# First weights' parts made earlier, matrix parts loaded over 15 steps, and three more places for second weights, in a two-layer spectral and MLP kernel

## The chip, the cores and the metric

The kernel runs on one core of one Trainium2 chip. The metric is the device time of one execution in microseconds; before the change it is 2771.64 us, the median of three runs (2771.27 to 2773.43). The engines are TensorE (PE, with its weight loads as PEld), VectorE (DVE), ScalarE (ACT), GpSimd (POOL) and the queue from which all DMAs are issued (SP). Each engine works through its own instructions in program order. An instruction that needs another engine's result, or a place that another still reads, waits on a semaphore, and everything behind it on that engine waits too.

## The reference

The input x has 2048 tokens (S) of 576 features (D). Two layers follow each other, with the same weights in both:

```python
x = x + _A_ref(_layernorm(x), ...)     # y = Cr @ (z @ Dr.T) - Ci @ (z @ Di.T), with z the normalized x
x = x + _B_ref(_layernorm(x), ...)     # y = gelu(layernorm(z) @ w1 + b1) @ w2 + b2
x = x + _A_ref(_layernorm(x), ...)
x = x + _B_ref(_layernorm(x), ...)
```

Cr and Ci are 2048 x 2048 (the sequence matrices), Dr and Di 576 x 576 (the hidden matrices), w1 is 576 x 4608, w2 is 4608 x 576; all of it is float32.

## The kernel before

**Arithmetic.** Every operand of a matmul is cut into a high and a low part (`split`, or an ACT copy followed by a DVE subtraction), and a product is three matmuls: high by high, high by low, low by high (`PASSES`). The large products use a Strassen-like scheme with seven block products in place of eight (`ORDER`, `OUTER`), so sums and differences of blocks have to be made as well.

**Stages.** For each layer:

- *Sequence products* (`Sequence`). `fill` normalizes x and makes the right sides. `run` then goes through 14 token tiles t of 128 rows (the first two are done in `first_mms`), each with seven products i of 24 matmuls of 288 columns, 98 in all. In each of the 98 steps DVE and ACT also prepare the cell (high and low part of a block of Cr and Ci) that is used some steps later: `high` (line 554), `low`, and the block sums `sums`. `post` moves results on and stores a token tile's product UV to DRAM.
- *Token-tile stage* (`hidden`, from line 777), for half 0 and half 1 of the tokens, eight tiles each. For each tile UV is transposed on PE (`turn`, line 764), multiplied with the nine 128-row parts of the hidden matrices (`dd`), added to x, normalized (`norms`) and transposed again (`turn_y`, line 834). The matrix parts are made in layer 0, half 0, and stored (`keep_d`); the three later times they are loaded, 576 KB for each of the nine.
- *MLP of that half* (`mlp`). 18 feature tiles q, worked in nine pairs g. `inner(q)` is a tile's first product: seven block products (the orders of `ORDER`) of seven matmuls, 512 columns wide, 49 matmuls, then gelu. `outer(g, i, side)` is one second product: two halves jj of 12 matmuls of 288 columns, 24 in all. In a pair's turn stand inner(2g), then outer(g-1) for i = 1, 6, 5, 3 (96 matmuls), inner(2g+1), then outer(g-1) for i = 7, 4, 2 (72). The last pair has outer only (g = NG).

**Weights' parts.** The seven block combinations of w1, each in high and low part, are made once, by the generator `weights()` (lines 247 to 294), in the background. A *step of the maker* is one resumption: low part of one combination (DVE subtraction of 384 columns, its store to `w1s`, for four of seven combinations a POOL sum or difference of 384 columns, and at times a load of raw w1) and high part of the next (two ACT copies). It takes 129 resumptions to its end. `pump()` is one resumption; `tick(share)` resumes in `share` of four calls. Before, `Sequence.run` calls tick(3) after each of the 98 products, and `inner` calls tick(2) after each of the seven orders. All of this falls into layer 0, half 0; afterwards the background is empty and both calls do nothing. When the maker ends, it frees its staging place, columns 0 to 1920 of the memory R.

The seven combinations of w2 are made in the MLP of layer 0, half 0, for pair g during turn g+1 (`make`, `due`, `advance`; hi is ACT, line 957, lo is DVE with a store to `w2s`). They go straight into the places that outer reads (`c2`). All later MLPs load them from `w2s`, 576 KB each, whenever a place is idle (`load_w`).

**Places.** In half 0, `c2` has two places, and a third (`give1`) when two of the seven places of first weights (`c1`) are given up. In half 1 it has three from the start. Taking and giving is first in, first out, in program order.

**Loads for half 1.** `Hidden.steps` (from line 685) is a generator that `outer` resumes in the last pair (g = NG-1), once for each jj, 14 times. It places the UV tiles and the matrix parts into the memory of Y, which is free when the last `inner` is done.

The program on SP is the order in which these calls are made; nothing reorders it.

Of the kernel before, what the change touches and what calls it, by code (L numbers as in the profile page):

```python
# [16 lines left out]
NT = S // P  # L17
# [136 lines left out]
def spectral_mixer(ctx: ExitStack, tc: tile.TileContext, x, dh, c0, cs, w1, b1, w2, b2, out):  # L154
# [149 lines left out]
    def tick(share):  # L304

        ticks[0] += 1
        if ticks[0] * share % 4 < share:
            pump()
# [6 lines left out]
    class Sequence:  # L315
# [286 lines left out]
        def run(self, hidden):  # L602
            for p in range(NP):
                while self.ready <= p:
                    next(self.pieces)
                self.first_mms(p)

            for _ in self.pieces:
                pass
            hidden.reserve()  # L610
            if not self.early:

                for k in range(KH):
                    dma(dhd[k], dh[k])
            steps = self.steps
            self.low(*steps[1])
            self.high(*steps[2])
            for t in range(PLAIN):
                self.first_post(t)
            for n, (t, i) in enumerate(steps):  # L620
                self.load_c()
                if n + 2 < len(steps):
                    self.low(*steps[n + 2])
                if i == 2 and t + 1 < NT:
                    self.sums(t + 1)
                self.load_c()
                if n + 3 < len(steps):
                    self.high(*steps[n + 3])
                self.mms(t, i)
                self.post(t, i)  # L630
                if t == NT - 1:
                    hidden.begin(self, ORDER.index(i))
                tick(3)
            for k in range(2):
                self.L[k].free()
            self.own.close()
            for z in self.Z:
                z.free()
            hidden.take()


    class Hidden:
# [41 lines left out]

        def steps(self):
            self.uvs = Slots(R, 2, 2 * D, Y_AT[0])
            self.X = A.place(X_AT[1], NT * DH)
            self.places = [R.place(Y_AT[0] + 4 * D + k * 2 * D, 2 * D) for k in range(KH)]

            def load_d(k):  # L690
                b = self.places[k].at
                self.load_d(k, Block(R, b, D), Block(R, b + D, D))

            self.load(0)
            load_d(0)
            yield
            self.load(1)
            load_d(1)
            for k in range(KH):
                yield  # L700
                if k + 2 < KH:
                    load_d(k + 2)
                self.high_d(k)
                if k:
                    self.low_d(k - 1)
            yield
            self.low_d(KH - 1)
            drain(self.turn(0, R.place(UT_AT[1][0], 2 * KH * P)))
            self.load_uv(2)
            yield  # L710
# [66 lines left out]
    def hidden(h, mlp):  # L777
# [74 lines left out]
        for n in range(NP):  # L852
            h.load(n + 2)
            for k in (n,) if n < NP - 1 else (n, n + 1):
                h.keep_d(k)
            if n:
                drain(turn(n + 1), *ln)
            if n == NP - 3:
                next(mlp)
            o = space()  # L860
            if n == NP - 1:

                h.uvs.close()
                next(mlp)
                o, ring = pp[0], [2, 3] * 3
            u = h.ut.pop(n)
            for k in range(KH):
                if n == 0 and k == KH // 2:
                    drain(turn(1))
                for m, (a, b) in enumerate(PASSES):  # L870
                    for e in range(2):
                        mm(o[:, e, :DH], u(2, KH, P)[:, a, k], h.dd[k][b](2, DH)[:, e],
                           k == 0 and m == 0, k == KH - 1 and m == 2)
            u.free()
            clock[0] += 1
            tile_x = xv[:, :, order[n]]
            add(nc.vector, tile_x, o[:, :, :DH], tile_x)
            if n >= 3 and n % 2:
                rests((n - 3) // 2)
            g = norms(n)  # L880
            next(g)
            ln = [g]
            if n >= 3 and n % 2:
                y_steps = turn_y((n - 3) // 2)
                if n < NP - 1:
                    drain(y_steps)


        for _ in range(3):
# [21 lines left out]
    def mlp(hid, store, first, after):  # L911
# [186 lines left out]
        def outer(g, i, side):  # L1098
            for jj in range(2):
# [14 lines left out]
                work(slot[0] % 3 < 2 or g >= last - 1)  # L1114
                slot[0] += 1
                advance()
                if g == last:
                    next(after, None)
                to = goal[i][:, 2 * jj:2 * jj + 2]
                if i == 6 and g == 0:  # L1120
# [24 lines left out]
        for g in range(NG + 1):  # L1145
# [2 lines left out]
                due.extend(make(g - 1))  # L1148
            if g == NG:
                work(99)  # L1150
                c1.close()
                hs.close()
                Y.free()
            for f in range(2):
                if g < NG:
                    for _ in inner(2 * g + f, None if g or f else 1):
                        pass
                if g:
                    advance(6 + 15 * f)
                    at[0] = 7 + 15 * f  # L1160
                    slot[0] = 0
                    for i in OUTER[f]:
                        outer(g - 1, i, 1 - f)
# [81 lines left out]
```

## Time and profile before

| what | value |
|---|---|
| runs (median, lowest, highest) | 2771.64, 2771.27, 2773.43 us |
| profiled execution: its own time | 2771.1 us |
| its span, first to last instruction | 2769.3 us |
| mean granted TensorE clock | 0.995 |
| DMA | 543.74 MB, mean 196 GB/s |

A line of the profile gives the kernel line, the engine, the operation, out<-in by the program's names, sizes (partitions x elements), a count and busy time. L194 and L191 are the helpers `sub` and `add`, L201 the helper `mm`, L188 the helper `dma`, so that all subtractions have one line, and the sizes tell them apart. R and A are the two large memories, bank is the accumulators, w_parts stands for both `w1s` and `w2s`. In a row of stretches stand, after the stretch and its length, the busy time of PE, PEld, DVE, ACT and POOL, each with its count of instructions, the granted share of the TensorE clock, the share of DMA engines busy and GB/s. Square brackets at the end of a row of the timeline hold the wait ahead of the instruction and what ended it. Neighbouring instructions of a stretch's edge are counted with it, so that the 49 matmuls of a first product are shown as 50 to 52.

The stages begin at these times of the span: sequence products of layer 0 at 67.7 us, token tiles of half 0 at 376.6, MLP at 464.2, token tiles of half 1 at 908.0, MLP at 996.2; sequence products of layer 1 at 1469.1, token tiles of half 0 at 1777.0, MLP at 1864.2, token tiles of half 1 at 2271.2, MLP at 2359.5.

### The profile page before, as it was taken

The numbers are of one execution on the slowest core, as the hardware profiler recorded it, in microseconds if no ns is written. First come the engines' busy times: TensorE is split into PE (matmuls) and PEld (weight loads), VectorE is DVE, ScalarE is ACT, GpSimd is POOL, SyncE is SP. The second block draws the span as 40 slices with busy tenths as digits, with TensorE's granted clock in tenths as the row PEclk, the third lists the DMA queues.
The fourth block names the chain that finished last, engine by engine and source line by source line (L and its number), as shares of the span: only waits on it lengthen the run. The fifth ranks groups of instructions, "written<-read, shape, count | busy, mean of one in ns | idle before, by whom it ended". The sixth has DMA issues, their size and how long they took to land.

```text
span 2769.3 us, 45580 instructions
## 1 busy us (share of the span) xinstructions
PE 2684.4 (97%) x17596; PEld 2513.2 (91%) x17596; DVE 1756.6 (63%) x2566; ACT 1087.4 (39%) x1850; POOL 791.9 (29%) x762
## 2 busy tenths in 40 slices
PE   7999999999999999999989999999999999999999
PEld 7999998788888988989889999998999989998988
DVE  8788866777776465555577666555555544655555
ACT  6555544544443243333254333334333313433331
POOL 5222223544534332222251000042222224221222
PEclk9999999999999999999999999999999999999999
DMA  5666675777776546666553333526666663566664
GB/s 198 240 222 223 231 257 172 268 263 271 263 262 216 216 152 195 192 196 192 168 206 119 124 126 125 187 98 208 194 195 192 189 247 132 185 194 195 191 197 152
DMA packets 208712, 543.74 MB, mean 196 GB/s; under 512 B 21985, under 2 KB 56801, under 8 KB 208353
## 3 DMA queue, kind: packets, MB, share of 16 engines
q1 hardware_dynamic: 208496, 540.84, 58.7%
q8 instruction: 139, 2.28, 0.3%
q14 instruction: 77, 0.62, 0.1%
HBM read 428.69 MB, written 114.72 MB: 196 GB/s over the span
## 4 chain that ended last, share of the span: by engine, by line
PE 69%; DVE 5%; issue 3%; DMA 3%; POOL 2%; ACT 1%; SPq 0%; POOLq 0%; DVEq 0%; ACTq 0%
PE bank L201 68%; DVE R L194 2%; DMA R<-w_parts 1%; DVE A L191 1%; POOL A L194 1%; DMA A<-x_mid 1%; PE bank L764 1%; POOL R L194 1%; DMA w_parts<-R 0%; DVE bank L191 0%; DVE A L194 0%; DVE moments L216 0%; DVE moments L231 0%; ACT R L957 0%; ACT R L1073 0%
## 5 line engine op out<-in xcount | busy, mean ns | idle before, releaser
L201 PE MATMUL bank<-R 128*128 128x288 f32 (+2 forms) x16972 | 2624.9, 316 | 72.3 <-DVE A L191 23.3
L201 PEld LDWEIGHTS bank<-R 128*128 128x128 f32 x16972 | 2447.5, 189 | 240.9 <-DVE A L191 30.3
L191 DVE TENSOR_TENSOR A<-bank,A 128x576 f32<-128x576 f32 (+3 forms) x808 | 567.4, 710 | 613.5 <-PE bank L201 533.6
L194 POOL TENSOR_TENSOR R<-A,R 128x512 fp32r<-128x512 f32 x288 | 374.3, 1310 | 981.5 <-ACT R L1073 948.6
L194 DVE TENSOR_TENSOR R<-A,R 128x1024 fp32r<-128x1024 f32 (+4 forms) x449 | 447.3, 1024 | 44.7 <-ACT R L554 25.4
L191 POOL TENSOR_TENSOR A<-A 128x576 f32<-128x576 f32 (+2 forms) x102 | 131.1, 1287 | 639.0 <-ACT A L592 349.6
L1013 ACT ACTIVATE bank<-bank,b1t 128x512 f32<-128x512 f32 (+1 forms) x224 | 144.8, 646 | 373.8 <-DVE bank L191 253.6
L194 DVE TENSOR_TENSOR R<-bank,R 128x512 fp32r<-128x512 f32 (+4 forms) x408 | 251.6, 636 | 59.7 <-ACT R L197 50.2
L1073 ACT ACTIVATE R<-A 128x512 fp32r<-128x512 f32 x288 | 176.2, 628 | 276.4 <-DVE A L194 117.3
L554 ACT ACTIVATE R<-A 128x1024 fp32r<-128x1024 f32 x196 | 204.0, 1054 | 135.4 <-DVE A L194 105.5
L191 DVE TENSOR_TENSOR bank<-bank,A 128x512 f32<-128x512 f32 (+1 forms) x228 | 152.2, 670 | 152.1 <-PE bank L201 151.7
L194 POOL TENSOR_TENSOR A<-A 128x288 f32<-128x288 f32 (+2 forms) x170 | 200.6, 1193 | 154.9 <-DVE R L194 83.9
L197 ACT ACTIVATE R<-bank 128x512 fp32r<-128x512 f32 (+2 forms) x160 | 74.1, 514 | 185.6 <-PE bank L764 129.3
L1073 ACT ACTIVATE R<-bank 128x512 fp32r<-128x512 f32 x216 | 120.7, 595 | 32.0 <-PE bank L201 32.0
L194 DVE TENSOR_TENSOR A<-A 128x1024 f32<-128x1024 f32 (+2 forms) x116 | 127.7, 1106 | 4.3 <-ACT A L241 1.2
L1040 ACT ACTIVATE A<-bank 128x512 f32<-128x512 f32 (+1 forms) x76 | 43.7, 575 | 211.6 <-PE bank L201 208.9
L241 ACT ACTIVATE A<-A,moments 128x576 f32<-128x576 f32 x64 | 54.0, 868 | 113.0 <-POOL moments L224 80.7
L194 DVE TENSOR_TENSOR A<-bank,A 128x512 f32<-128x512 f32 x144 | 98.2, 682 | 0.0
L594 DVE SCALAR_TENSOR_TENSOR A<-A 128x288 f32<-128x288 f32 x28 | 18.4, 657 | 88.4 <-POOL A L191 88.4
L1013 ACT ACTIVATE A<-bank,b1t 128x512 f32<-128x512 f32 (+1 forms) x76 | 50.4, 663 | 54.8 <-DVE bank L191 54.8
L268 ACT ACTIVATE R<-A,power,middle 128x128 fp32r<-128x128 f32 x126 | 60.8, 483 | 0.0
L222 POOL TENSOR_TENSOR moments<-moments,power 128x1 f32<-128x1 f32 x32 | 17.6, 551 | 148.3 <-DVE moments L219 148.3
(50 smaller groups left out, 632.4 us busy)
## 6 DMA issues: line engine op xcount, KB each, us to landing
R<-w_parts SPq DMA_DIRECT2D x504, 320.0 KB, 3.3
R<-w_parts SPq DMA_DIRECT2D x189, 576.0 KB, 3.7
A<-in_cs SPq DMA_DIRECT2D x112, 512.0 KB, 4.3
w_parts<-R SPq DMA_DIRECT2D x126, 320.0 KB, 3.7
w_parts<-R SPq DMA_DIRECT2D x63, 576.0 KB, 4.0
uv_mid<-A SPq DMA_DIRECT2D x32, 576.0 KB, 2.8
A<-in_w SPq DMA_DIRECT2D x72, 192.0 KB, 3.8
R<-dh_parts SPq DMA_DIRECT2D x23, 576.0 KB, 10.5
```

The costliest lines, as they stand in the source:

```text
L191: engine.tensor_tensor(dst, a, b, op=op)
L194: engine.tensor_tensor(dst, a, b, op=OP.subtract)
L197: nc.scalar.activation(hi, src, AF.Copy)
L201: nc.tensor.matmul(o, a, b, start=start, stop=stop, skip_group_check=True)
L241: nc.scalar.activation(dst, src, AF.Identity, bias=mv[:, 4:5], scale=mv[:, 3:4])
L268: nc.scalar.activation(t[:, 2], src[:, 1], AF.Identity, bias=power[:, 2:3], scale=middle)
L554: nc.scalar.activation(self.cells[t, i](2, NP, P)[:, 0], self.source(t, i), AF.Copy)
L594: nc.vector.scalar_tensor_tensor(uv[:, 1, 0], p7, -1.0, u, op0=OP.mult, op1=OP.subtract)
L764: nc.tensor.transpose(at, v[:, k], ident)
L1013: nc.scalar.activation(dst, src, AF.Gelu_apprx_tanh, bias=bias(f))
L1040: nc.scalar.activation(up, o, AF.Copy)
L1073: nc.scalar.activation(H[q, k](2, TC)[:, 0], src, AF.Copy)
```

## The change

There are three parts.

1. The maker's steps. `Sequence.run` resumes the maker after every one of the 98 products (before after three in four), and `hidden` resumes it twice at the end of each token tile. In the MLP `inner` still resumes it after every second order, for as long as it lasts.
2. Loads for half 1. `Hidden.steps` is resumed six times in the second group of the second-to-last pair's turn (outer(NG-2), i = 7, 4, 2) and then 14 times as before. First come the first UV tile and the nine matrix parts, one for each resumption, with the second UV tile after the third; then the two x tiles; the transposition of UV tile 0 stands in the 17th resumption, one order's half earlier than before. `high_d` and `low_d`, which did nothing when the parts are only loaded, are no longer called. To have room, the memory of Y and the places of first weights are given up right after the last `inner`, and no longer at the start of the last turn.
3. Places for second weights in half 0. A fourth one is taken at columns 0 to 1152 of R as soon as these are free (in layer 0 when the maker has ended, in layer 1 from the first turn), and two more in the memory of the first weights when those are given up.

```diff
@@ Sequence.run
-                tick(3)
+                pump()
@@ Hidden.steps
             self.uvs = Slots(R, 2, 2 * D, Y_AT[0])
-            self.X = A.place(X_AT[1], NT * DH)
             self.places = [R.place(Y_AT[0] + 4 * D + k * 2 * D, 2 * D) for k in range(KH)]
-
-            def load_d(k):
+            self.load_uv(0)
+            for k in range(KH):
                 b = self.places[k].at
                 self.load_d(k, Block(R, b, D), Block(R, b + D, D))
-
+                yield
+                if k == 2:
+                    self.load_uv(1)
+            self.X = A.place(X_AT[1], NT * DH)
             self.load(0)
-            load_d(0)
             yield
             self.load(1)
-            load_d(1)
-            for k in range(KH):
+            for _ in range(6):
                 yield
-                if k + 2 < KH:
-                    load_d(k + 2)
-                self.high_d(k)
-                if k:
-                    self.low_d(k - 1)
-            yield
-            self.low_d(KH - 1)
             drain(self.turn(0, R.place(UT_AT[1][0], 2 * KH * P)))
@@ hidden, end of each token tile
+            pump()
+            pump()
@@ mlp, outer
-                if g == last:
+                if g == last or half == 0 and g == last - 1 and side == 0:
                     next(after, None)
@@ mlp, turns
             if g == NG:
                 work(99)
-                c1.close()
                 hs.close()
-                Y.free()
+            if half == 0 and len(c2.idle) < 4:
+                more = R.place(0, 4 * DH)
+                if more:
+                    c2.idle.append(more)
             for f in range(2):
                 if g < NG:
                     for _ in inner(2 * g + f, None if g or f else 1):
                         pass
+                if g == last and f:
+                    c1.close()
+                    Y.free()
+                    if half == 0:
+                        c2.idle += [R.place(C1_AT[0] + k * 4 * DH, 4 * DH) for k in range(2)]
```

## The prediction

> **What bounds the kernel now.** The first page gives the balance of the engines, and the stretches of the span, cut at the first matmul of each stage, give the place of every loss.
>
> ```profile
> span 2769.3 us, 45580 instructions
> PE 2684.4 (97%) x17596; PEld 2513.2 (91%) x17596; DVE 1756.6 (63%) x2566; ACT 1087.4 (39%) x1850; POOL 791.9 (29%) x762
> ```
>
> TensorE (PE) is the bound, so a change can win only where PE waits or runs slowly. The same work stands in the span twice, once for each layer, which gives a yardstick: layer 0 makes weights' parts beside it, layer 1 doesn't. The view of busy time by stretch, columns PE, PEld, DVE, ACT, POOL, granted clock, DMA share and GB/s:
>
> ```profile
> 67.71:376.59 308.88, 308.58 (x2329) 308.11 (x2330) 252.72 (x275) 168.80 (x304) 74.44 (x54) 1.00 0.68 230
> 1469.09:1777.01 307.92, 307.92 (x2329) 307.92 (x2329) 196.78 (x204) 119.34 (x158) 11.69 (x14) 1.00 0.38 136
> 376.59:464.20 87.61, 84.34 (x656) 82.79 (x655) 48.72 (x105) 32.88 (x67) 33.95 (x58) 1.00 0.53 184
> 908.87:996.16 87.29, 83.74 (x648) 81.96 (x647) 44.37 (x96) 27.57 (x58) 33.39 (x57) 1.00 0.43 149
> 464.20:907.97 443.77, 412.79 (x2381) 364.36 (x2378) 319.17 (x462) 204.75 (x390) 195.10 (x143) 0.99 0.74 262
> 1864.19:2271.21 407.02, 401.53 (x2380) 363.60 (x2378) 228.12 (x344) 130.52 (x219) 98.49 (x77) 1.00 0.64 202
> ```
>
> Rows 1 and 2 are the sequence products of layers 0 and 1: the maker's steps beside layer 0 cost PE 1 us. Rows 3 and 4 are the token-tile stage without and with nothing of the maker either. Rows 5 and 6 are the MLP of half 0: 443.77 against 407.02 us, a loss of 36.8 us in layer 0. Cut finer, in three parts and by single products:
>
> ```profile
> 464.20:515.11 50.91, 44.12 (x254) 37.67 (x251) 36.73 (x61) 29.17 (x61) 24.52 (x20) 1.00 0.82 282
> 1864.19:1906.32 42.13, 42.13 (x253) 38.02 (x251) 27.37 (x46) 20.22 (x37) 11.70 (x10) 1.00 0.68 205
> 634.41:646.89 12.48, 11.63 (x51) 9.23 (x50) 8.88 (x11) 7.38 (x15) 7.40 (x6) 1.00 0.63 218
> 828.40:839.98 11.58, 11.58 (x52) 9.30 (x51) 6.48 (x9) 5.59 (x9) 5.88 (x4) 1.00 0.57 192
> 854.51:866.06 11.55, 11.51 (x52) 9.15 (x50) 5.53 (x8) 4.35 (x7) 0.00 (x0) 1.00 0.54 186
> 1972.42:1983.80 11.38, 11.38 (x52) 9.32 (x51) 4.14 (x6) 3.64 (x6) 2.54 (x2) 1.00 0.70 204
> 866.06:907.97 41.91, 33.56 (x218) 32.12 (x216) 24.29 (x32) 9.36 (x15) 17.88 (x13) 0.88 0.69 260
> 2235.05:2271.21 36.16, 30.87 (x217) 30.20 (x216) 17.39 (x25) 4.79 (x9) 11.40 (x9) 0.95 0.81 309
> ```
>
> The start (tiles 0 to 2) loses 50.91 - 42.13 = 8.8 us; the end loses 41.91 - 36.16 = 5.8 us; what lies between, 515.11 to 866.06 against 1906.32 to 2235.05, loses 350.95 - 328.73 = 22.2 us. Rows 3 to 6 are single first products (the 49 matmuls of one feature tile). With the maker's steps one takes 12.48 us, and PE is busy for 11.63 of them; tiles 16 and 17, after the maker has ended, take 11.58 and 11.55 although the second weights are still made beside them; in layer 1 it is 11.38. So 0.91 us of a product is the maker, 0.2 the second weights.
>
> **The change, part by part.**
>
> *Maker's steps.* It needs 129 resumptions. Before, three in four sequence products give 73, and every second of 7 orders in a tile gives 3.5 per tile, so tiles 0 to 15 carry the other 56. After, 98 sequence products give 98, eight token tiles 16, and 15 are left for tiles 0 to 4. Twelve first products (4 to 15) lose their steps, the last few of them not wholly burdened: 12 x 0.91 = 10.9, of which I take **-10**, since the lighter of them (tile 15, half empty) lost less. The 96 matmuls between them barely change (I take -1). Start: tiles 0 to 3 keep their steps, **0** (bounds -4 and +4, half of the 8.8 either way, because the steps fall on other orders).
>
> Where the steps go, the cost is DVE's. The window that is steady in both layers, and the groups in it:
>
> ```profile
> 100.00:370.00 270.00, 270.00 (x2045) 270.00 (x2044) 227.86 (x248) 147.59 (x262) 67.07 (x48) 1.00 0.67 226
> 1480.00:1750.00 270.00, 270.00 (x2044) 270.00 (x2043) 178.67 (x184) 104.87 (x135) 10.07 (x12) 1.00 0.35 124
> L194 DVE TENSOR_TENSOR R<-A,R 128x384 fp32r<-128x384 f32 x65 | 39.5, 608 | 0.6 <-issue 0.6
> L194 POOL TENSOR_TENSOR A<-A 128x384 f32<-128x384 f32 x27 | 40.0, 1480 | 57.7 <-DVE R L194 30.1 <-issue 23.0 <-DMA A<-in_w 4.1
> ```
>
> 65 steps cost DVE 227.86 - 178.67 = 49.2 us, 0.76 each, more than their own 0.61. The window holds 85 products, so 20 more steps make 227.9 + 15 = 243 us of 270 (90%); ACT goes from 147.6 by 20 x (147.59 - 104.87)/65 = 13 to 161. PE stays covered on average; in a token's seven products DVE has 2.2 us left of 22.2, and the first products, where the buffers fill, had already no reserve. I take **+2** (bounds 0 and +8, 0.6 per group of seven; it is nearer the row that shows 1 us at three quarters of the load). If the cover went, the 25 added steps would cost 25 x 0.76 = 19 us.
>
> In the token-tile stage two steps per tile add 1.5 us DVE, 1.3 us ACT and 1.7 us POOL (4 subtractions of 1.48 in 7 steps) to a tile of some 10 us in which DVE is busy 48.72/87.61 = 56%. They stand behind the tile's transposed parts and ahead of the next tile's, which have a 7 us product as cover; only at the last tile do they stand in a chain that PE waits for. I take **+2** (0 to +6).
>
> *End in layer 0.* PE's and ACT's instructions with the wait before each:
>
> ```profile
> 876.87 0.40 PE L201 MATMUL bank<-R 128*128 128x288 f32 x1 [0.76 <-ACT R L957]
> 878.26 4.82 PE L201 MATMUL bank<-R 128*128 128x288 f32 x23 [0.99 <-DVE R L194]
> 885.55 11.40 PE L201 MATMUL bank<-R 128*128 128x288 f32 x84 [0.19 <-DVE A L191]
> 902.91 5.22 PE L201 MATMUL bank<-R 128*128 128x288 f32 x24 [5.96 <-DVE A L191]
> 894.21 0.69 ACT L957 ACTIVATE R<-A 128x576 fp32r<-128x576 f32 x1 [6.01 <-DMA w_parts<-R]
> 900.63 0.68 ACT L957 ACTIVATE R<-A 128x576 fp32r<-128x576 f32 x1 [5.73 <-DMA w_parts<-R]
> 888.25 0.91 SPq L188 DMA_DIRECT2D w_parts<-R  x1
> ```
>
> The last high parts wait for their place, whose earlier content is still being stored: that store was issued at 888.25 among the matrix loads and landed at 900.6. With three places more, six in all, the seven parts of the last pair reuse one place only, and that one was stored first, some 20 us earlier. The matrix loads also begin one group sooner. So the 5.96 us goes, and with it the slowness after it: 24 matmuls in 5.22 us (0.22 each) against 84 in 11.40 (0.136), 1.9 us. **-7.9**. The first waits (0.76 and 0.99, and slow matmuls behind them) hang on the last pair's making and stay; they are late next.
>
> *End in layer 1.*
>
> ```profile
> 2258.79 8.04 PE L201 MATMUL bank<-R 128*128 128x288 f32 x48 [4.17 <-DMA R<-w_parts]
> 2267.93 3.44 PE L201 MATMUL bank<-R 128*128 128x288 f32 x24 [1.11 <-DMA R<-w_parts]
> 2230.00:2240.00 10.00, 10.00 (x61) 9.08 (x60) 5.93 (x10) 4.24 (x7) 0.39 (x1) 1.00 0.07 17
> 2250.00:2260.00 10.00, 5.83 (x40) 5.62 (x40) 2.92 (x4) 0.00 (x0) 0.00 (x0) 0.93 1.04 412
> R<-w_parts SPq DMA_DIRECT2D x189, 576.0 KB, 3.7
> R<-dh_parts SPq DMA_DIRECT2D x23, 576.0 KB, 10.5
> ```
>
> Two of the last second weights land late, behind matrix parts on a full path (412 GB/s), while ten us earlier it moved 17. After, the parts start with the group before (from 2235), and each second weight is issued ahead of the part in its step. Of SP's issues from 2235 to the last second weight there are 16 of 576 KB (six weights, eight parts, two UV tiles): 9.4 MB, 22.9 us at 412 GB/s and some 2 more to land (3.7 median, 1.4 of it its own transfer), so about 2260, and PE needs it at 2263.5 (216 matmuls at 270/2045 = 0.132 after 2235). The waits go (4.17 + 1.11 = 5.3), and the slow matmuls after them (48 in 8.04 against 0.13 each: 1.8): **-7.1**. The two x tiles, now last, land at 2264 and are added after the next product.
>
> *What stays out.* Layer 1's other stages issue the same instructions; closing the first weights' places one group sooner frees memory that nobody takes before.
>
> Sum: -10 - 1 + 0 + 2 + 2 - 7.9 - 7.1 = **-22.0 us**. The profiled execution took 2771.1 us (span 2769.3), beside a median of 2771.6, so the sum needs no correction: 2771.1 - 22.0 = **2749 us**.
>
> **A rule weighed against a row.** Two rows of the sequence stage, DVE and POOL:
>
> ```profile
> 246.96 1.88 DVE L194 TENSOR_TENSOR R<-A,R 128x1024 fp32r<-128x1024 f32 x1 [0.35 <-ACT R L554]
> 251.98 1.22 DVE L194 TENSOR_TENSOR R<-A,R 128x1024 fp32r<-128x1024 f32 x1
> 246.73 1.02 POOL L194 TENSOR_TENSOR A<-A 128x384 f32<-128x384 f32 x1 [4.15 <-DMA A<-in_w]
> ```
>
> The same subtraction takes 0.66 us longer when a POOL subtraction has begun before it. The Trainium skill ("SBUF — State Buffer", section "Who interferes with whom") states that a DVE instruction with two SBUF inputs and a GpSimd instruction that reads SBUF exclude each other for a whole instruction. With that rule these rows agree, and it speaks against the change: each added POOL subtraction may hold DVE for all of its own length. Worked by it, 20 more steps in the window bring 11 POOL subtractions of 1.48 and 20 x 0.61 of their own, 28 us: 256 of 270, still covered on average, and the same sum; packed into one place of the group it is rival 1.
>
> **Rivals.**
>
> 1. *The sequence products become DVE's* (slower than before). Seven steps per seven products lock each POOL subtraction to the same DVE instructions in every token tile. At the dearest, each of the 4 subtractions in 7 steps delays two DVE instructions by 0.66 and up to 0.8: 4 x (0.6 + 1.5) + 3 x 0.6 = 10.2 us on top of 178.67/270 x 22.2 = 14.7 gives 24.9 us for 22.2, +2.7 in each of 14 groups: +38 - 2 in place of +2, **2785**. It beats the gains from 23.9 us, a mean of 1.3 us per step. Against it: the mean of 65 steps is 0.76. Chance 0.07.
> 2. *Small stalls in both stages* at their bounds, +8 and +6: **2759**. For it: the full load at the start of the sequence; against: 1 us at three quarters. Chance 0.16.
> 3. *The ends stay bound by transfers.* At that stretch's mean of 309 GB/s the last second weight lands at 2267.5, 4 us late; with as much in layer 0 the ends give 6 in place of 15: **2758**. Chance 0.12.
> 4. *Rivals 2 and 3 together*, or the start grows by its bound as well: **2768**, within 0.2% (5.5 us, about what a measurement of this kernel can tell from no change). Chance 0.05.
> 5. *More is freed*: the start loses 4 less, no cost in sequence and token tiles, and the fourth place takes the second weights' 0.2 us off each product: **2738**. Chance 0.08.
>
> **How the numbers follow.** The forecast, 2743 to 2755, has 0.52. Rivals 2, 3 and 5 are faster too: 0.88 faster, 0.05 the same, 0.07 slower. The range leaves out rival 1, rival 4 and the edges of 2 and 5: **2737 to 2763**.
>
> **What would show it.** Right: the sequence stage of layer 0 at 309 to 312 us with DVE near 285; first products 4 to 15 at 11.5 to 11.6 us; no wait of ACT L957 on a store near 890; no PE wait for w_parts before the second token stage of layer 1, and that MLP at 400 us in place of 407. Wrong: PE waits on DVE R L194 in every group of seven products; a token-tile stage over 94 us; or those first products still at 12 us, which would mean that the second weights, and not the maker, hold DVE.

## The result and the profile after

The changed kernel takes 2776.5 us (median of 14 runs, 2773.42 to 2780.36), the one before it, run beside it, 2771.23 us (14 runs, 2769.78 to 2773.43): a ratio of 1.002 with a 95% interval of 1.0012 to 1.0028. It is slower by 0.2%; forecast were 2749 us, 2737 to 2763. The profiled execution of after took 2780.24 us, 3.7 above its own median, with a span of 2778.5 against 2769.3.

Cut at the same places (the first matmul or transposition of a stage, and for the last stage the last matmul), the two profiled spans differ like this:

| stage | before, us | after, us | difference |
|---|---|---|---|
| layer 0: sequence products | 308.9 | 327.7 | +18.8 |
| token tiles, half 0 | 87.6 | 100.9 | +13.3 |
| MLP, half 0 | 443.8 | 423.2 | -20.6 |
| token tiles, half 1 | 88.2 | 89.9 | +1.7 |
| MLP, half 1, and layer 1's start | 472.9 | 474.7 | +1.8 |
| layer 1: sequence products | 307.9 | 309.1 | +1.2 |
| token tiles, half 0 | 87.2 | 87.1 | -0.1 |
| MLP, half 0 | 407.0 | 398.4 | -8.6 |
| token tiles, half 1 | 88.3 | 89.8 | +1.5 |
| MLP, half 1 | 402.8 | 402.8 | 0 |

The differences add up to +9.0 of the 9.2 us. Of the two half-1 token stages some 1.6 us are no loss: the first transposition now stands 12 matmuls earlier, so these count with the token tiles and no longer with the MLP ahead of them. The rows of after that answer to those shown of before, busy time by stretch with the same columns (the fifth is a single first product, tile 6):

```profile
67.84:395.54 327.70, 314.55 (x2328) 309.49 (x2329) 281.97 (x298) 183.42 (x351) 82.89 (x69) 1.00 0.71 248
395.54:496.48 100.94, 88.66 (x657) 86.86 (x655) 58.23 (x124) 46.34 (x102) 44.99 (x65) 0.95 0.73 239
496.48:919.68 423.20, 406.55 (x2368) 361.52 (x2366) 286.75 (x420) 177.45 (x308) 165.39 (x120) 1.00 0.66 235
1880.47:2278.85 398.38, 398.17 (x2368) 360.49 (x2366) 227.32 (x343) 130.42 (x219) 97.09 (x76) 1.00 0.65 206
614.44:625.80 11.36, 11.36 (x52) 9.31 (x50) 6.51 (x9) 5.59 (x9) 5.88 (x4) 1.00 0.58 193
100.00:370.00 270.00, 260.92 (x1934) 256.80 (x1933) 239.83 (x252) 151.82 (x289) 69.51 (x58) 1.00 0.72 246
```

Both MLPs won about what was forecast. The two stages that took the steps lost 32 us together where 4 were forecast. In the last row, the steady part of the sequence products, PE does 1934 matmuls in 270 us where before it did 2045, while DVE is busy for 239.83 us, 89%: it isn't full, and yet PE waits.

*Sequence products.* PE's timeline in after, with the wait before each row in square brackets, and DVE's waits from 100 to 370 us (total, times, longest):

```profile
213.28 22.80 PE L201 MATMUL bank<-R 128*128 128x288 f32 x168 [0.73 <-DVE R L194]
236.93 22.94 PE L201 MATMUL bank<-R 128*128 128x288 f32 x168 [0.85 <-DVE R L194]
260.75 22.60 PE L201 MATMUL bank<-R 128*128 128x288 f32 x168 [0.88 <-DVE R L194]
```

```profile
DVE A L191 <- issue: 18.0, 12, 1.9
```

PE waits once in every seven products (168 matmuls), for a low part by DVE, and the group has become 23.8 us long (236.93 to 260.75) in place of 22.2. DVE itself stands still once in every group as well, ahead of the block sums (L191 on 1024 columns); "issue" means that the profile names nothing that it waited for. DVE and SP in one group:

```profile
238.87 1.23 DVE L194 TENSOR_TENSOR A<-A 128x1024 f32<-128x1024 f32 x1
...
245.48 1.23 DVE L191 TENSOR_TENSOR A<-A 128x1024 f32<-128x1024 f32 x1 [1.81 <-issue]
246.74 1.22 DVE L194 TENSOR_TENSOR A<-A 128x1024 f32<-128x1024 f32 x1
247.88 4.93 DVE L194 TENSOR_TENSOR R<-A,R 128x384 fp32r<-128x384 f32 x4
...
258.76 1.93 DVE L194 TENSOR_TENSOR R<-A,R 128x1024 fp32r<-128x1024 f32 x1 [0.30 <-ACT R L554]
...
262.69 1.22 DVE L194 TENSOR_TENSOR A<-A 128x1024 f32<-128x1024 f32 x1
```

```profile
240.12 0.33 SPq L188 DMA_DIRECT2D A<-in_cs  x1
```

and the group of these loads from 100 to 370 us (count, size, median us from issue to landing):

```profile
A<-in_cs SPq DMA_DIRECT2D x45, 512.0 KB, 4.7
```

Read as a ring: DVE's subtraction at 238.87 is the last reader of a block and frees its place at 240.1; SP issues the next block's load there at 240.12; this one lands at 245.40, 5.3 us later; the sums, which need the block, start at 245.48 after a wait; then DVE works almost without a pause to the low part at 258.76, for which PE waits until 260.7; at 262.69 stands the next freeing of the same kind. The parts add up to the group: 1.25 us to the load's issue, 5.36 to the sums and 17.21 to the next freeing, 23.8 us. PE is no member of this ring. That was the first reading; the experiments test it.

*Token tiles.* PE's and SP's timelines in after, then SP's waits in the stage, after and before:

```profile
411.14 7.43 PE L201 MATMUL bank<-R 128*128 128x288 f32 x54
421.97 2.16 PE L757 MATMUL bank<-ident,A 128*128 128x128 f32 x9 [3.40 <-DMA A<-uv_mid]
423.79 8.19 PE L201 MATMUL bank<-R 128*128 128x288 f32 x54
...
454.88 1.17 PE L757 MATMUL bank<-ident,A 128*128 128x128 f32 x9 [2.11 <-DVE moments L219]
455.81 8.84 PE L201 MATMUL bank<-R 128*128 128x288 f32 x54
```

```profile
412.81 0.32 SPq L188 DMA_DIRECT2D w_parts<-R  x1
413.23 0.41 SPq L188 DMA_DIRECT2D A<-in_w  x1
413.73 0.39 SPq L188 DMA_DIRECT2D w_parts<-R  x1
414.17 0.44 SPq L188 DMA_DIRECT2D A<-in_w  x1
414.70 0.74 SPq L188 DMA_DIRECT2D A<-uv_mid  x1
```

```profile
SPq L188 <- DVE R L194: 53.6, 12, 10.3
```

```profile
SPq L188 <- DVE R L194: 7.5, 3, 3.1
```

The load of the UV tile that PE transposes at 421.97 is issued only at 414.70, behind two of the maker's stores, and lands 7.2 us later. The stores (w_parts<-R) wait for the low parts, and DVE computes these after all else of the tile. Everything behind them in SP's queue waits too: 53.6 us of waits for DVE in the stage, against 7.5 before. Two later tiles (444.41 and 454.88) start with waits of 2 us in the same place. The trace names DVE as the one waited for, but the UV loads that SP issued at 437.38 and 448.11 land at 444.27 and 454.75, 0.14 and 0.13 us before PE goes on, so that it is these loads.

*Ends of the MLPs.* PE in the last turn, layer 0 and layer 1:

```profile
897.23 3.31 PE L201 MATMUL bank<-R 128*128 128x288 f32 x23 [0.99 <-DVE R L194]
902.51 14.47 PE L201 MATMUL bank<-R 128*128 128x288 f32 x96 [1.97 <-DVE A L191]
917.99 1.85 PE L201 MATMUL bank<-R 128*128 128x288 f32 x12 [1.01 <-DVE A L191]
...
2239.80 39.21 PE L201 MATMUL bank<-R 128*128 128x288 f32 x256
```

The wait of 5.96 us has gone from layer 0, and layer 1 has none left at all.

### The profile page after: what moved, and what is told of

Read it like the earlier page. It is cut to its first block, busy times and chain, and to the rows that moved or that the text cites. A ratio compares the mean times of both kernels' runs of the same rounds, so it can differ in the third digit from the quotient of the medians.

```text
span 2778.5 us, 45549 instructions
## 1 busy us (share of the span) xinstructions
PE 2687.4 (97%) x17596; PEld 2514.4 (90%) x17596; DVE 1764.0 (63%) x2566; ACT 1088.1 (39%) x1850; POOL 783.6 (28%) x762
## 3 DMA queue, kind: packets, MB, share of 16 engines
q8 instruction: 139, 2.28, 0.3%
## 4 chain that ended last, share of the span: by engine, by line
PE 75%; issue 8%; DVE 7%; DMA 4%; POOL 3%; ACT 2%; SPq 0%; DVEq 0%; POOLq 0%; ACTq 0%
PE bank L201 74%; DVE R L194 3%; POOL A L194 1%; POOL A L191 1%; DVE A L194 1%; DVE A L191 1%; PE bank L757 1%; ACT R L554 1%; DMA R<-w_parts 1%; DMA A<-uv_mid 1%; DVE moments L231 1%; DMA w_parts<-R 0%; SPq L188 0%; DMA A<-in_cs 0%; DVE moments L216 0%
## 5 line engine op out<-in xcount | busy, mean ns | idle before, releaser
L191 DVE TENSOR_TENSOR A<-bank,A 128x576 f32<-128x576 f32 (+3 forms) x808 | 567.5, 710 | 625.8 <-PE bank L201 552.9
L194 POOL TENSOR_TENSOR R<-A,R 128x512 fp32r<-128x512 f32 x288 | 376.8, 1319 | 1063.4 <-ACT R L1068 1022.8
L194 DVE TENSOR_TENSOR R<-A,R 128x1024 fp32r<-128x1024 f32 (+4 forms) x449 | 453.4, 1038 | 40.4 <-ACT R L554 23.3
L191 POOL TENSOR_TENSOR A<-A 128x576 f32<-128x576 f32 (+2 forms) x102 | 135.8, 1333 | 566.8 <-ACT A L592 312.7
L194 DVE TENSOR_TENSOR R<-bank,R 128x512 fp32r<-128x512 f32 (+4 forms) x408 | 251.2, 635 | 56.0 <-ACT R L197 50.2
L191 DVE TENSOR_TENSOR bank<-bank,A 128x512 f32<-128x512 f32 (+1 forms) x228 | 152.7, 670 | 157.9 <-PE bank L201 157.5
L194 POOL TENSOR_TENSOR A<-A 128x288 f32<-128x288 f32 (+2 forms) x170 | 183.9, 1090 | 160.8 <-DVE R L194 57.5
L194 DVE TENSOR_TENSOR A<-A 128x1024 f32<-128x1024 f32 (+2 forms) x116 | 123.5, 1070 | 4.0 <-ACT A L241 0.9
L194 DVE TENSOR_TENSOR A<-bank,A 128x512 f32<-128x512 f32 x144 | 97.9, 680 | 0.0
L267 ACT ACTIVATE R<-A 128x256 fp32r<-128x256 f32 x126 | 51.8, 411 | 100.8 <-DMA A<-in_w 34.8
L594 DVE SCALAR_TENSOR_TENSOR A<-A 128x288 f32<-128x288 f32 x28 | 24.0, 856 | 69.5 <-POOL A L191 69.5
```

The costliest lines, as they stand in the source:

```text
L191: engine.tensor_tensor(dst, a, b, op=op)
L194: engine.tensor_tensor(dst, a, b, op=OP.subtract)
L267: nc.scalar.activation(t[:, 1:4:2], src[:, 0:3:2], AF.Copy)
```

## The experiments

Theories at the start: **1**, each loss belongs to the place where the steps stand, and the MLPs' gains are as forecast; **1a**, in the token tiles it is SP's queue; **2**, in the sequence products it is the ring through the load of a block. The rival to 2 is that of the prediction: DVE and GpSimd hold each other up, and the stage is DVE's. All kernels are the changed one with the edit shown (e12 apart, see there); of longer edits only the lines that matter stand here. The ratios are to the kernel before, run beside each (its medians: 2773.45 for e1 to e4, 2774.69 for e5 to e8, 2773.39 for e9 to e12, 2772.54 for e13 and e14). The stages are those of layer 0, from one profiled execution each. That one took between 4.4 us less (e9) and 7.8 us more (e3) than its kernel's median, so a few us of a stage can belong to the execution; of e2, e6, e8, e13 and e14, on which the reading of the sequence products rests, it is within 1.3 us of the median.

| kernel | median, us | ratio, 95% interval | sequence | token tiles | MLP, half 0 |
|---|---|---|---|---|---|
| e1_no_steps | 2760.31 | 0.9939 [0.9924, 0.9954] | 308.6 | 87.7 | 436.0 |
| e2_seq_only | 2776.18 | 1.0004 [0.9995, 1.0013] | 330.0 | 89.2 | 430.2 |
| e3_tiles_only | 2760.57 | 0.9938 [0.9920, 0.9956] | 308.7 | 100.7 | 432.2 |
| e4_tiles_ahead | 2774.57 | 0.9996 [0.9986, 1.0006] | 329.9 | 91.8 | 423.6 |
| e5_phase | 2763.27 | 0.9959 [0.9944, 0.9974] | 316.8 | 88.9 | 431.6 |
| e6_no_pool | 2752.08 | 0.9920 [0.9905, 0.9935] | 309.5 | 87.9 | 427.4 |
| e7_in_shadow | 2801.80 | 1.0097 [1.0082, 1.0112] | 357.1 | 87.1 | 430.9 |
| e8_sums_later | 2759.76 | 0.9951 [0.9934, 0.9967] | 312.2 | 89.3 | 431.4 |
| e9_all_three | 2757.38 | 0.9939 [0.9927, 0.9952] | 311.8 | 92.0 | 423.6 |
| e10_two_later | 2764.98 | 0.9971 [0.9962, 0.9980] | 323.3 | 91.6 | 427.0 |
| e11_loads_only | 2764.21 | 0.9969 [0.9957, 0.9981] | 308.7 | 87.7 | 441.3 |
| e12_places_only | 2763.19 | 0.9964 [0.9950, 0.9977] | 308.7 | 87.3 | 439.4 |
| e13_seventh | 2761.02 | 0.9960 [0.9946, 0.9974] | 314.5 | 89.1 | 431.3 |
| e14_all_and_seventh | 2758.22 | 0.9950 [0.9935, 0.9965] | 315.2 | 92.1 | 423.6 |

### Which part costs what

**e1_no_steps**: the maker's steps as before, the rest of the change kept. **e2_seq_only**: only the tiles' steps taken out (the second hunk). **e3_tiles_only**: only the first hunk.

```diff
@@ Sequence.run
-                pump()
+                tick(3)
@@ hidden, end of each token tile
-            pump()
-            pump()
```

> Part 1 undone (the maker resumed after three in four products, not at all in the token tiles), parts 2 and 3 kept. Theory 1 (the added steps cost 19 us in the sequence products and 13 in the token tiles, and the rest of the change does what was forecast): both stages as before the change (308.9 and 87.6 us), the MLP of half 0 436 us in layer 0 and 400 in layer 1, in all 2756. Rival (the ends gain only because the MLP runs without the maker): the end of layer 0 keeps its wait, 2764.

> The two resumptions of a token tile left out, one per sequence product kept. Theory 1 (losses belong to the stage in which the steps stand): sequence products 328 us, token tiles 87.6, MLP of half 0 in layer 0 429 us (31 steps left, tiles 0 to 8 carry them); in all 2769. Rival (the maker's backlog at the end of the sequence is what slows the token tiles): token tiles still over 95 us.

> Three in four resumptions in the sequence products, the two of each token tile kept. Theory 1: sequence products 309 us, token tiles 101, MLP of half 0 in layer 0 432 us (40 steps left); in all 2765. Rival (the token tiles lose only because the sequence ends late): token tiles 90 us, 2754.

Each stage loses where the steps stand: 308.6 without and 330.0 with them in the sequence products, 87.7 and 100.7 in the token tiles (89.2 in e2, which has none there). Theory 1 holds. What the steps bring in the MLP is 436.0 - 423.2 = 12.8 us, less than either of the stages' losses in the profiles. The loss in the sequence products is in the medians too: 2776.18 for e2 against 2760.31 for e1. That in the token tiles is there only in part. e3's profiled execution is its slowest (2768.4 us, the others 2758.6 to 2762.1), and by the medians e3 takes 0.3 us more than e1, although its MLP gains 436.0 - 432.2 = 3.8; so the tiles' steps cost some 4 us in its usual execution, an estimate from these four numbers, and not 13.

### The token tiles' queue

**e4_tiles_ahead**: the two steps stand ahead of the tile's product, so that their stores no longer wait behind the tile's own work on DVE.

```diff
@@ hidden, each token tile, ahead of the product
+            pump()
+            pump()
             u = h.ut.pop(n)
@@ hidden, end of each token tile
-            pump()
-            pump()
```

> The whole change, but a tile's two resumptions stand ahead of the tile's product (after its transposition) and no longer behind it. Theory 1a (a tile's loss comes from the DMA queue: the next but one tile's UV load stands behind the maker's stores, which wait for DVE after the product): token tiles 88 to 91 us, in all 2765. Rival 1b (it is the added DVE, ACT and POOL work, wherever it stands): token tiles 101 us, 2776.

PE in e4, the fifth tile to the sixth:

```profile
439.21 1.69 PE L827 MATMUL bank<-ident,A 128*128 128x128 f32 x14
440.74 0.93 PE L837 MATMUL bank<-ident,A 128*96 128x128 f32 x7
441.50 1.15 PE L757 MATMUL bank<-ident,A 128*128 128x128 f32 x9
443.31 7.66 PE L201 MATMUL bank<-R 128*128 128x288 f32 x54 [0.66 <-DVE R L194]
```

The waits for UV have gone, and with the same 16 steps the stage takes 91.8 us in place of 100.9. In e3, where the steps stand as in the change, the trace names the loads themselves:

```profile
PE bank L757 <- DMA A<-uv_mid: 7.2, 3, 3.8
```

Theory 1a holds for what the profiles show. In the whole time it is worth less: the median, 2774.57, missed the expected 2765 and is 1.9 us below the change's 2776.50, where the two profiled stages differ by 9. Against the kernels run beside them the change is 5.3 us slower and e4 1.1. How long the UV waits are in the usual execution isn't known. The 4 us that remain in e4's stage are what the steps cost even so, within the 0 to 6 that the prediction allowed.

### The ring of the sequence products

All from e5 to e8 leave the tiles' steps out, as e2 does, and compare with its 330.0 us.

**e5_phase**: three steps ahead of the first product, so that all later ones stand three places on in the maker's own period of seven.

```diff
+            for _ in range(3):
+                pump()
             for n, (t, i) in enumerate(steps):
                 self.load_c()
```

> As e2_seq_only (one resumption per sequence product, none in the token tiles), but the maker has three steps' start, so that its four POOL sums fall behind the products 4, 1, 6 and 2 of the group of seven in place of 2, 5, 7 and 3. Theory 2 (the sequence products are bound by a cycle of DVE and a load: from the place that DVE frees after the third product's block, a load of 5.3 us to the next group's block sums, then 15.2 us of DVE with the POOL sums beside it, and 3.3 us to the next freeing, 23.8 us for 22.2 of PE): with two of the four POOL sums outside the 15.2 us, sequence products 314 us, in all 2760. Rival (it is the sum of DVE's work, wherever it stands): 330 us as in e2, 2776.

The stage falls by 13 us, and its steady part has no wait left. As many steps, in the same places among the products (and three more ahead of them), so the number of steps alone isn't the cause: it is which step stands where.

**e6_no_pool**: the maker's GpSimd sums left out.

```diff
-            if then:
-                then()
```

> As e2_seq_only, with the maker's POOL sums and differences left out, so that four of the seven block combinations of w1 are wrong. Theory 2: without them beside DVE the 15.2 us become about 12.7, the cycle 21.3 us, under PE's 22.2: sequence products 309 to 310 us, in all 2755. Rival (SP's queue with the maker's stores and loads, which are all still there): 325 to 330 us.

309.5 us. Its steady part, 100 to 370 us:

```profile
100.00:370.00 270.00, 270.00 (x2044) 270.00 (x2043) 216.34 (x267) 162.11 (x303) 9.71 (x12) 1.00 0.78 261
```

With 12 GpSimd instructions in place of 58 beside it DVE's 267 instructions take 216.34 us, 0.81 each; in after it is 239.83/252 = 0.95. So the GpSimd sums lengthen the ring's string of DVE work, and both theories allow this result; it doesn't tell them apart.

**e7_in_shadow**: the seven steps of a group unevenly spread: five behind the first two products, just ahead of the sums, where DVE waits for the load, and two later.

```diff
-                pump()
+                for _ in range((2, 3, 0, 1, 0, 1, 0)[n % 7]):
+                    pump()
```

> As e2_seq_only, but the seven resumptions of a group of seven products stand 2, 3, 0, 1, 0, 1, 0 behind the products, so that five of them fall into the time in which DVE waits for the load. Theory 2: three steps of 0.6 to 0.9 us leave the 15.2 us, the cycle is 21.5 to 22.2 us: sequence products 309 to 313 us, in all 2757. Rival (DVE's total): 330 us.

A miss: 357.1 us, the slowest of all. DVE's, ACT's and PE's waits in e7, 100 to 370 us:

```profile
ACT R L267 <- DMA A<-in_w: 54.4, 12, 6.5
DVE R L194 <- ACT R L268: 50.0, 26, 5.5
...
PE bank L201 <- DVE R L194: 21.8, 11, 3.8
```

Steps one after another have to wait for the load of raw w1, whose place a step shortly before has freed. ACT waits for that load, DVE for ACT (50.0 us), PE for DVE: read so, a second ring of the same kind, inside the maker. Steps don't only cost their instructions, they need the distance between them.

**e8_sums_later**: the block sums one product later, so that the load has 3 us more.

```diff
-                if i == 2 and t + 1 < NT:
+                if i == 5 and t + 1 < NT:
                     self.sums(t + 1)
```

> As e2_seq_only, but the next group's block sums stand one product later (in the fourth of the seven), with the same work in all. Theory 2: DVE has other work while the load lands, the cycle loses its wait of 1.8 us and is 22.0 to 22.3 us: sequence products 309 to 314 us, in all 2758. Rival (DVE's total, or the lock alone): 326 to 330 us.

312.2 us, as theory 2 expected, with every step in place and every GpSimd sum kept.

### Together, and one product further

**e9_all_three**: the whole change, with the edits of e4 and e8. **e10_two_later**: the same with `i == 7`, the sums two products later.

> The whole change with the two cures that worked one by one: the block sums one sequence product later, and the token tile's two steps ahead of its product. If the losses are separate (theories 1a and 2), they add up: sequence stage 311 to 313 us, token-tile stage of half 0 91 to 93, the MLP after it 423 to 424, and the whole 2760 (the run with the sums later alone) - 7.8 (MLP 431.4 to 423.6) + 2.5 (token tiles 89.3 to 91.8) = about 2754.5, range 2752 to 2757. If one cure feeds the other's loss, it stays at 2760 or above.

> The same with the block sums two sequence products later in place of one. Theory 2 (what costs is that the sums stand right behind the landing of a load whose place DVE itself has freed late): two products later nothing of the cycle is left, sequence stage 309 to 312 us, the whole within 3 us of the run with one product. Rival (DVE is simply full, and the sums now stand 6 us nearer to the low part that needs them): over 314 us.

e9 adds up as expected by stages (311.8, 92.0, 423.6); its median of 2757.38 is just outside the range that was set; its profiled execution (2752.95), from which the stages come, is inside it and the fastest of the five. e10 is a miss for theory 2 as it was put: 323.3 us, over the 314 that the rival had set. Its waits of ACT, then of DVE, 100 to 370 us:

```profile
ACT R L267 <- DMA A<-in_w: 33.6, 11, 4.5
...
DVE R L194 <- ACT R L268: 26.9, 12, 3.8
```

DVE no longer waits ahead of the sums; it waits once a group for ACT, and ACT for raw w1, as in e7. The sums' new place has closed the maker's ring. But "DVE is full" isn't borne out either, since DVE stands idle for 2.2 us in each of these groups. What was left open was whether the dependence of the load on DVE makes the loss at all.

**e13_seventh**: a seventh place for blocks, with all of the work where e2 has it (the products' UV has one place less).

```diff
+            more = A.place(AN - 9 * NP * P + 0, NP * P)
+            self.idle.append(more)
```

> The change without the token tiles' steps, and a seventh place for blocks of Cr and Ci in the sequence products, so that a block's load is issued one giving of a place earlier (some 3 us or more) and no longer waits for DVE's latest subtraction. The work of DVE, ACT and POOL is the same. Theory 2 (a cycle: DVE gives a place late, the load lands 5 us after that, DVE's next string of work starts late): the sequence stage falls from 330 to 309-314 us, the whole to 2757-2760. Rival (DVE and POOL simply hold each other up, 90% of the time being too much): the stage stays at 325 or above. The products' UV has one place in place of two, a wait of ACT for its store would cost under 1 us per group.

PE, and the steady part of e13:

```profile
87.04 294.82 PE L201 MATMUL bank<-R 128*128 128x288 f32 x2208 [3.62 <-ACT A L590]
```

```profile
100.00:370.00 270.00, 270.00 (x2045) 270.00 (x2044) 251.55 (x269) 161.42 (x305) 71.28 (x60) 1.00 0.76 254
```

From 87 us on PE runs 2208 matmuls without one wait. DVE is busy for 251.55 of 270 us, 93%, more than the 89% at which after loses 1.6 us in each group, and the same GpSimd work stands beside it. Theory 2 set 309 to 314 for the stage, the rival 325 or above; it is 314.5, and the median of 2761.02 is likewise just over the 2757 to 2760 expected. The steady part settles it against the rival: not the load of DVE, but the time at which the block's load could be issued. What is left of the stage's loss stands at its start: the wait of 3.62 us before that row, for an ACT copy (L590), and slow matmuls behind it (18 in the 4 us from 88 to 92, at a granted clock of 0.50). ACT itself had waited for raw w1:

```profile
83.02 0.42 ACT L267 ACTIVATE R<-A 128x256 fp32r<-128x256 f32 x1 [8.52 <-DMA A<-in_w]
```

In e2 this wait of ACT is 6.1 us and PE's is 1.31. With the seventh place SP issues four loads of blocks, and not three, ahead of those of raw w1; that this is the difference is read from the order and not tested.

**e14_all_and_seventh**: e9 with the seventh place.

> The seventh place together with the block sums one product later and the token tiles' steps ahead of the product. Theory 2: 311.8 us of the sequence stage fall to 309-311, the whole to 2755 (range 2752 to 2758), that is, the cycle is broken already and the place adds little. Rival: what remains of the loss comes from the same loads, and it falls by 3 us.

315.2 us against 311.8 for e9, and a median of 2758.22 against 2757.38; expected were 309 to 311 and 2755. The place adds nothing once the sums stand later, and costs what it costs in e13 (PE's wait at the start is 3.65 us). Nothing of the ring was left in e9, whose steady part is:

```profile
100.00:370.00 270.00, 270.00 (x2044) 270.00 (x2044) 251.10 (x271) 160.18 (x304) 77.81 (x61) 1.00 0.76 259
```

### The ends

Both have the maker's steps as in e1. **e11_loads_only** leaves out the three places, **e12_places_only** takes the loads as before.

```diff
@@ e11
-            if half == 0 and len(c2.idle) < 4:
-                more = R.place(0, 4 * DH)
-                if more:
-                    c2.idle.append(more)
@@ e11
-                    if half == 0:
-                        c2.idle += [R.place(C1_AT[0] + k * 4 * DH, 4 * DH) for k in range(2)]
@@ e12
-                if g == last or half == 0 and g == last - 1 and side == 0:
+                if g == last:
```

(e12 also takes `Hidden.steps` of before.)

> The earlier loads for half 1 and the earlier giving up of Y, without the three more places for second weights and with the maker's steps as before the change. Theory (the end of layer 0 hangs on the places, the end of layer 1 on the loads): layer 0's last turn keeps its wait of ACT L957 for a store, MLP of half 0 in layer 0 about 441 to 444 us; layer 1's MLP of half 0 about 398 to 400. Rival (the places make both): layer 1's stays at 405 or above.

> The three more places for second weights, with the loads for half 1 and the maker's steps as before the change. Theory: MLP of half 0 in layer 0 about 436 to 438 us (the wait for the store goes), in layer 1 403 to 406 (a little better than 407, because second weights can be fetched further ahead, but the matrix parts still crowd the last turn). Rival (the places make both ends): 398 to 400 in layer 1.

Layer 0: from the end of tile 17's product to the same matmul, before takes 41.9 us, e11 36.3, e12 36.3, and after 36.3. Either part alone takes the wait away. ACT in e11 still waits for a store:

```profile
900.32 0.69 ACT L950 ACTIVATE R<-A 128x576 fp32r<-128x576 f32 x1 [3.23 <-DMA w_parts<-R]
```

but PE no longer feels it. Layer 0's MLP is 441.3 us in e11, as expected, and 439.4 in e12, over the 436 to 438 set for it. Layer 1's MLP of half 0 is 407.0 before, 401.9 in e11 (1.6 of it the moved matmuls, so -3.5) and 399.7 in e12, which has no wait left:

```profile
2223.66 38.53 PE L201 MATMUL bank<-R 128*128 128x512 f32 x257
```

Here the rival came out: the places alone make the whole gain of that end, and the earlier loads add nothing to it. They are worth something elsewhere: e12's half-1 token stage of layer 0 takes 90.1 us where before takes 88.2, with a wait of PE of 1.7 us for UV, and e1, which has loads and places, is at 2760.31 us where e12 is at 2763.19.

## Why the prediction was wrong

- *First products 4 to 15 and the 96 matmuls between, -10 and -1*: right in sum. Tiles 4 to 15 take 140.6 us after 148.8 (-8.2; the row of tile 6 shows 11.36, but tiles 9, 11 and 13 still take 12.4 to 12.6, tile 9 behind a wait of 0.99 for a second weight), and what stands between and behind them, the groups of 96 above all, gives 4 where 1 was taken (-12.3 together). Why tiles 11 and 13 stay slow is open.
- *Start, 0*: -1.1.
- *End of layer 0, -7.9*: mis-sized, -5.6. The wait of 5.96 went, but waits of 1.97 and 1.01 for DVE came in its place.
- *End of layer 1, -7.1*: -7.0 (8.6 less the 1.6 of moved matmuls). The size was right and the reason only half so: more places, not earlier loads, as e12 shows. That the size fits so well is in part luck.
- *Sequence products, +2 (0 to +8)*: **the step that failed**, +18.8. "PE stays covered on average; in a token's seven products DVE has 2.2 us left of 22.2" was true and didn't decide. The average forecast for DVE was 243 of 270 us; e13 and e9 run at 251 with PE never waiting. The step took a share of busy time for the whole condition and left out what DVE itself has to wait for. What decided was the dependence of a load on DVE's own last reader, 5.3 us of load and 17.2 us from the sums to the next freeing: with the freeing subtraction a ring of 23.8 us.
- *Token tiles, +2 (0 to +6)*: **failed too**, +13.3 in the profiled execution: PE waits 9.0 us longer there and its matmuls take 4.3 us longer (88.66 against 84.34). The sum priced DVE, ACT and POOL and left out the stores and loads that the two steps put into SP's queue, ahead of the next UV load. e4 shows that the priced part was right (+4). Since the profiled execution is 3.7 us above its median, and e3's median tells of some 4 us only, the size in the usual execution is open, and may lie within the bounds.
- *Rival 1* had the right place (PE waits on DVE L194 in every group) and the right consequence. That the 23.9 us per group from which it would decide is near the measured 23.8 is luck, since its mechanism, DVE as the bound, isn't the one. The rule that it stood beside is that of the Trainium skill ("SBUF — State Buffer", section "Who interferes with whom"): DVE with two SBUF inputs and a reading GpSimd exclude each other. The runs agree with it: e9 has DVE at 251.1 us with 49 more GpSimd instructions than e6 and four more of DVE's own, 251.1 - 216.3 - 4 x 0.81 = 31.5 us, 0.64 per GpSimd instruction, the 0.66 of the prediction's rows. That overlap lengthens the ring; e13 shows that it doesn't make the loss.
- Of the marks named for "wrong", two were seen: PE waits on DVE R L194 in every group, and a token-tile stage over 94 us.

With the measured sizes the sum is -12.3 - 1.1 + 18.8 + 13.3 - 5.6 - 7.0 = +6.1. The rest to +9.2 is 1.8 us in the MLP of half 1 of layer 0 with the start of layer 1, in which no instruction was moved, and 1.2 in layer 1's sequence products; e9 to e14 have between 0.6 and 1.9 of the first. The cause of that stays open. So does why e7's and e10's second ring, through raw w1, closes just there: no kernel with a further place for raw w1 was run.

The best versions that do all the work are e9 at 2757.38 us, e14 at 2758.22, e8 at 2759.76 and e1 at 2760.31; e9 and e1 have the same ratio (0.9939), so that their 2.9 us are not told from nothing. So most of what was had here lies in the places and loads of the ends; the moved steps bring 12.8 us in the MLP and, even cured, give back 3 us and 4 us where they now stand.

## What to carry to other kernels

Before work is moved under another engine's cover, follow each load that the cover needs back to what frees its place: if that is the engine which gets the work, load latency plus the work between is a ring, and the ring, not the engine's share of busy time, has to be shorter than the cover. List a moved step's DMAs too: in an in-order queue a store that waits for a late result holds up every load behind it. When such a ring is found, one more place (e13) or a use one product later (e8) takes most of its loss away with the work where it was moved; whether the move pays then is a second question, and here these two (2761.02 and 2759.76 us) did no better than undoing it (e1, 2760.31).

## What the runs showed of the hardware

A wait of 2 us can cost TensorE more than its own length. After the wait of 2.11 us at 454.88 the matmuls first run at full rate, then slowly, then fast again; the stretches of after, where the third number from the end is the granted clock:

```profile
452.00:456.00 4.00, 1.89 (x16) 1.68 (x16) 2.90 (x7) 1.25 (x3) 0.99 (x2) 1.00 0.88 302
456.00:458.50 2.50, 2.50 (x13) 2.50 (x12) 1.48 (x3) 1.66 (x4) 2.40 (x4) 0.53 0.91 311
461.00:464.00 3.00, 3.00 (x26) 3.00 (x25) 0.00 (x0) 0.00 (x0) 0.00 (x0) 1.00 0.99 334
```

13 matmuls in 2.50 us at a granted clock of 0.53, beginning 1.3 us after PE had started again, against 26 in 3.00 us at 1.00. That product takes 8.84 us where the one of 411.14 takes 7.43, so the wait cost 1.4 us more. After the wait of 1.98 us before 444.41 nothing of the kind is seen. The granted clock is halved in three stretches of this stage, after the waits of 3.40, 2.11 and 2.28 us (the last before 486.91):

```profile
422.03:425.44 3.41, 3.41 (x16) 3.41 (x17) 0.69 (x1) 2.39 (x5) 2.26 (x4) 0.50 1.06 333
456.17:459.58 3.41, 3.41 (x17) 3.41 (x16) 1.58 (x3) 1.52 (x3) 3.39 (x6) 0.50 0.91 285
486.88:490.29 3.41, 3.38 (x16) 3.35 (x17) 3.35 (x8) 2.16 (x5) 0.58 (x2) 0.50 0.91 275
```

Each is 3.41 us long, and they begin 34.14 and 30.71 us apart, ten and nine times that. The Trainium skill ("TensorE: Matmul & The Clock Gate", section "What's actually happening") tells of a free-running window of some 3.4 us, after an idle one of which the clock is halved. The length, the distances and the delayed start agree with such a window, but here 2.1 and 2.3 us without a matmul sufficed; why the wait of 1.98 us had no effect is not shown.
